# Row-tiled decay spreads, a quarter of two chunks' masked products on GpSimd, and re-placed gate, store and sum steps in a fused SSD and expert-merge kernel

## The chip, the cores and the metric

The kernel runs on one core of a Trainium2 chip. The metric is the device time of one execution in microseconds, as the median of several runs. Everything is in fp32.

## What is computed

The reference has two parts, joined by a reshape. The first is a chunked state-space layer (Mamba-2 SSD) over 4 sequences of 768 tokens with 8 heads of 32 values and a state of 16. Cut to what matters:

```python
L = np.exp(cum[:, :, :, None] - cum[:, :, None, :]) * causal   # decays inside a chunk
M = np.einsum('bhin,bhjn->bhij', Cc, Bc) * L                   # scores times decays
y = M @ xc + (Cc @ state) * exp(cum)
state = decay_full * state + sum_j(Bc[j] x[j] * decay_from_j)
```

The second takes the 3072 tokens of 256 values through four two-layer experts and adds them up with normalized gates:

```python
p = domain_probs / (domain_probs.sum(-1, keepdims=True) + 1e-09)
for e in range(E):
    h = np.maximum(x @ w1[e], 0.0)
    out += p[:, e:e + 1] * (h @ w2[e])
```

## The kernel before

**Tiles.** Tokens come in 24 chunks of 128 (the kernel may choose its own chunk length, since the recurrence is the same). Four chunks, one of each sequence, make a block of 512 tokens; there are six blocks. The experts are worked through in steps: eight steps a block (four experts, two halves of the hidden layer), 48 in all, numbered n. A step forms X and Y banks of the first layer (`fmul`, L480; in steps 0 and 1 `plain_first`, L533), turns them into gated hidden tiles on VectorE (`total`, L503; `gated`, L508; `diff`, L520), and multiplies these with w2 one step later (`smul`, L564; `plain_second`, L552). From step 2 on, a Strassen-like scheme with seven products in place of eight is used. It needs sums of the weight blocks (S1 to S4), which GpSimd makes in the first block (`sum_w1`, L186; `sum_w2`, L194: four operations of 128x256 at L180 to L184 and a store to DRAM for the later blocks, L192 and L198).

**One chunk of the first part.** `masks` (L375, ScalarE) cuts C into two masked copies, ctm. `scores` (L382, TensorE) multiplies them with B, in four row tiles of 32x128 (quarter q of the heads in rows 32q to 32q+31), into four banks g. `spread` (L315, TensorE, chunks 0 to 2 only) spreads the chunk's decay factors `a_q` over all 128 partitions into PSUM; later chunks load the spread factors from DRAM (`load_decays`, L123, from `acut_d`, which `store_decays` writes, L277). `decay_part` (L342) scans them on VectorE into the decay matrix LT (L366), and GpSimd makes the B columns of MT from it (L371). `masked` (L401, VectorE) multiplies g with LT into MT, one quarter of the heads at a time (L407). `outputs` (L411, TensorE) multiplies x with MT into y (L433), and ScalarE copies y into yT (L442) and, for the state, into A (L446 to L449).

For chunk 0, `spread` uses four row tiles (K = 32 rows each) in four banks. For chunks 1 and 2 it uses full 128-row matmuls with the stationary operand `qmask` (L332), two of 128x256 to a bank, two banks.

**The gates.** `turn_gates` (L285) transposes the normalized probabilities (pp, L289), ScalarE copies them to p_sb (L292), and SyncE stores them as p_d. `spread_gate` (L295) spreads the rows of one expert over all partitions (gp, L301), and ScalarE copies the result (L305). Without that tile the first `gated` can't run.

**What sets the order.** Nothing is scheduled by a planner: each engine takes its instructions in the order in which the program calls the functions, and waits on semaphores for its data and its buffers. The calls ahead of the loop over steps are L697 to L770. DMAs take turns on eight semaphores of the hardware queues, whichever engine issues them: an issue waits until the transfer eight turns earlier has landed. PSUM tiles are named by bank (X, Y, acc0 to acc3, and two rotating "att" banks); whoever takes a bank waits for the last reader of what was in it. `turn` (L690) multiplies ones into a bank that nobody reads.

Within a step of the loop (L775 to L869) the weight sums have two places: at mid-step, behind the second parts of the decays (L829 to L834), and at the end of the step (L858 to L863).

Of the kernel before, what the change touches and what calls it, by code (L numbers as in the profile page):

```python
# [8 lines left out]
FP32 = mybir.dt.float32  # L9
# [3 lines left out]
P = 128  # L13
NQ, NT = 4, 2
# [3 lines left out]
def kernel(  # L18
# [38 lines left out]
    nc = tc.nc  # L57
# [15 lines left out]
    SPB = E * JJ  # L73
# [7 lines left out]
    PLAIN = 2  # L81
# [192 lines left out]
    nc.gpsimd.tensor_copy(a_cut, a_sb)  # L274
    nc.gpsimd.memset(a_cut[:, :, 0:1], 0.0)

    def store_decays():  # L277
        nc.scalar.dma_start(
            out=acut_d.rearrange("c h s -> (c h) s").rearrange("(p r) s -> p r s", r=2), in_=a_cut)
        nc.scalar.dma_start(  # L280
            out=ac_d.rearrange("c h s -> (c h) s").rearrange("(p r) s -> p r s", r=2), in_=a_sb)

    gate = {}

# [27 lines left out]

    yT, yS = {}, {}

    def spread(c, halves=(0, 1)):  # L315


        s = st[c]
        if c == 0:
            s["a"] = []  # L320
            for q, (pool, tag) in enumerate(((ps_f, "X"), (ps_f, "Y"), (ps_s, "acc2"), (ps_s, "acc3"))):
                k = slice(32 * q, 32 * q + 32)
                b = pool.tile([P, NT * P], FP32, tag=tag, name="a")
                nc.tensor.matmul(
                    out=b, lhsT=ones[k], rhs=a_q[k, c].rearrange("p t s -> p (t s)"),
                    start=True, stop=True, tile_position=(32 * q, 0))
                s["a"].append(b)
            return
        for i in halves:
            b = ps_f.tile([P, 2, NT * P], FP32, tag="XY"[i], name="a")  # L330
            for q in range(2):
                nc.tensor.matmul(  # L332
                    out=b[:, q], lhsT=qmask[:, 2 * i + q, 0:1].to_broadcast([P, P]),
                    rhs=a_q[:, c].rearrange("p t s -> p (t s)"), start=(q == 0), stop=True,
                    skip_group_check=True)
            s.setdefault("a", []).append(b.rearrange("p q s -> p (q s)"))

    def decays(c):
        for part in range(3):
            decay_part(c, part)  # L340
# [60 lines left out]
    def masked(cs, rs):  # L401
        for r in rs:
            for c in cs:
                q = r ^ 2 * turned_round(c)
                h = slice(NT * q, NT * q + NT)
                s = st[c]
                nc.vector.tensor_mul(s["MT"][:, h, 0:P], s["g"][q], s["LT"][:, h])  # L407

    state = {}

    def outputs(cs):  # L411

        ys = {}
        for c in cs:
            k, i = divmod(c, CPB)
            ys[c] = y = ps_att.tile([P, NT, P + N], FP32, tag="att", name="y")
            if k > 0:
                for a_ in range(2):
                    rows = slice(HALF * a_, HALF * a_ + HALF)
                    to = HALF * (1 - a_ if turned_round(c) else a_)  # L420
                    nc.tensor.matmul(  # L421
                        out=y[to:to + HALF, :, 0:P],
                        lhsT=state[i][1].rearrange("p q d -> p (q d)")[rows, rows],
                        rhs=st[c]["cts"][rows], start=True, stop=False,
                        tile_position=(HALF * a_, to), skip_group_check=True)
        for c in cs:
            s, y = st[c], ys[c]
            k, i = divmod(c, CPB)
            w = P + N if k < NBLK - 1 else P
            for t in range(NT):  # L430
                for q in range(NQ):
                    h = NQ * t + q
                    nc.tensor.matmul(  # L433
                        out=y[32 * q:32 * q + 32, t, 0:w], lhsT=s["xb"][:, h * D:h * D + D],
                        rhs=s["MT"][:, NT * q + t, 0:w], start=(k == 0 and t == 0), stop=True,
                        tile_position=(0, 32 * q), skip_group_check=True)
        for c in cs:
            s, y = st[c], ys[c]
            k, i = divmod(c, CPB)
            if i == 0:  # L440
                yT[k] = ffn.tile([P, NT, BLK], FP32, tag="yT", name="yT")
            nc.scalar.copy(out=yT[k][:, :, i * P:i * P + P], in_=y[:, :, 0:P])  # L442
            if k < NBLK - 1:
                s["A"] = att.tile([P, NT, N], FP32, tag="A", name="A", bufs=4)
                if i % 2:
                    nc.scalar.copy(out=s["A"][:HALF], in_=y[HALF:, :, P:])  # L446
                    nc.scalar.copy(out=s["A"][HALF:], in_=y[:HALF, :, P:])
                else:
                    nc.scalar.copy(out=s["A"], in_=y[:, :, P:])  # L449
# [235 lines left out]


    homes = ((ps_s, "acc0"), (ps_s, "acc1"), (ps_att, "att"), (ps_att, "att"))
    banks = ((ps_s, "acc2"), (ps_s, "acc3"), (ps_s, "acc0"), (ps_s, "acc1"))

    def turn(n, w=4):  # L690

# [4 lines left out]

    turn(1)  # L697
    turn(1, 2)
    spread(0)
    turn(1, 3)  # L700
    masks(0)
    scores([0], homes)
    decays(0)
    masks(1)
    spread(1)
    store_decays()
    masks(2)
    masked([0], range(NQ))
    outputs([0])
    scores([1], banks)  # L710
    decays(1)
    turn_gates(ps_att, "att")
    spread(2, (0,))
    spread_gate(ps_att, "att")
    masked([1], range(NQ))
    outputs([1])
    spread(2, (1,))
    sum_w1(0, 0)
    load_decays(3)
    load_w2(1)  # L720
# [54 lines left out]
    for n in range(PLAIN, NS):  # L775
        k, r = divmod(n, SPB)

        ahead = CPB * (k + 1)
        scanned = [ahead + d for d in {0: [0], 2: [1], 4: [2], 5: [3]}.get(r, [])]
        scored = [ahead + d for d in {3: [0, 1], 6: [2, 3]}.get(r, [])]  # L780
        done = [ahead + d for d in {4: [0, 1], 7: [2, 3]}.get(r, [])]
        if k == NBLK - 1:
            scanned, scored, done = [], [], []
        ending = r == 0 and k > 0
        e = r // JJ
        if r % JJ == 0 and n + JJ < NS:
            load_gate(*divmod(n // JJ + 1, E))
        if PLAIN + 2 < n + 2 < NS:
            load_w1(n + 2)
            load_w2(n + 2)  # L790
        opened(n)
        total(n, 1, "11")
        gated(n, "11", "z11")
        for work in late:
            work()
        if r == 1 and k > 0:
            combine(k - 1, 0)
            combine(k - 1, 1)
        for c in scanned:
            decay_part(c, 0)  # L800
        for c in scored:
            masks(c)
        if k > 0 and 2 <= r < CPB + 2:
            leave(k - 1, r - 2)
        smul(n - 1, 1)
        fmul(n, 6)
        snap(n, 6)
        smul(n - 1, 3)
        if ending:
            keep(k - 1, 0)  # L810
        if done:
            outputs(done)
            states.extend(done)
        fmul(n, 5)
        fmul(n, 7)
        snap(n, 7)
        total(n, 7, "22")
        smul(n - 1, 7)
        smul(n - 1, 5)
        if ending:  # L820
            keep(k - 1, 1)
        gated(n, "22", "z22")
        if r == 1 and k > 0:
            combine(k - 1, 2)
        for c in scanned:
            decay_part(c, 1)
        for c in scored:
            decay_part(c, 2)
        if n == PLAIN:  # L829
            sum_w2(0, 1)  # L830
        elif n == SPB - 4:
            sum_w1(n + 2)
        elif n == SPB - 2:
            sum_w2(n)  # L834
        if n < CPB:
            load_chunk(n + CPB)
        for c in scanned if n >= CPB else []:
            if c + 2 < NCH:
                load_decays(c + 2)
        for c in done:  # L840
            if c + CPB < NCH:
                load_tokens(c + CPB)
                load_heads(c + CPB)
        fmul(n, 3)
        total(n, 6, "12")
        fmul(n, 4)
        gated(n, "21", "X")
        gated(n, "12", "z12")
        if r == SPB - 1 and k < NBLK - 1:
            sums(k + 1)  # L850
        smul(n - 1, 6)
        if scored:
            scores(scored, ((ps_att, "att"), (ps_att, "att"), (ps_f, "Y"), (ps_f, "X")))
            masked(scored, (3, 2, 0, 1))
        smul(n - 1, 2)
        diff(n, "T3", "22", "12")
        smul(n - 1, 4)
        if n == PLAIN:  # L858
            sum_w2(1, 1)
        if n != SPB - 4:  # L860
            sum_w1(n + 2)
        if PLAIN < n != SPB - 3:
            sum_w2(n + 1)  # L863
        diff(n, "T1", "12", "11")
        if r == 1 and k > 0:
            turned_out(k - 1)
        late = [lambda n=n: diff(n, "T2", "22", "T1"), lambda n=n: diff(n, "T4", "21", "T2")]
        if states:
            late.append(lambda c=states.pop(0): carry(c))  # L869
# [48 lines left out]
```

## Time and profile before

| what | value |
|---|---|
| median of 7 runs | 641.62 us (641.24 to 643.39) |
| profiled execution | 642.08 us, span 640.3 us |
| granted TensorE clock | 1.000 |
| TensorE, VectorE busy | 633.4 and 484.0 us |
| ScalarE, GpSimd busy | 118.4 and 108.5 us |
| first X matmul of step 0 | 14.69 us |
| waits of TensorE in the page's sense | 1.2, 1.1 and 0.6 us |

A row of a timeline gives the start in us, the length of the merged piece in us, the engine, the line, the operation, what is written and read, and how many instructions are merged; in square brackets stands the idle time before it and what ended it. One 128x256 fp32 matmul leaves two records. PE is TensorE's matmul, DVE VectorE, ACT ScalarE, POOL GpSimd, SP SyncE; a q behind the name means the engine's instruction queue. A piece's length includes the tail of its last instruction, so pieces overlap a little. In the list of waits a row tells who waited for whom, the total, how often, and the longest.

### The profile page before, as it was taken

Reading aid. Unit: us, or ns where it says so; the run is one execution under the profiler, and the core shown is the slowest. Engines: PE = TensorE matmul, PEld = TensorE weight load, DVE = VectorE, ACT = ScalarE, POOL = GpSimd, SP = SyncE. Lnnn points to the kernel's source line nnn. Section 1 sums busy time; section 2 is a strip of 40 time slices with the busy share of each in tenths; the row PEclk is TensorE's granted clock in tenths of the full one; section 3 lists DMA queues with packets and bytes.
Section 4 is the critical chain, followed back from the end, with each engine's and each line's share of the span. In section 5 each row is a group of like instructions: output and inputs, shape, how many; then the busy total and the mean of one; then the engine's idle time right before and its main releaser. Section 6 shows DMA issues by size and latency. Waiting matters only on the chain.

```text
span 640.3 us, 9224 instructions
## 1 busy us (share of the span) xinstructions
PE 633.4 (99%) x3407; PEld 538.4 (84%) x3407; DVE 484.0 (76%) x809; ACT 118.4 (18%) x257; POOL 108.5 (17%) x157
## 2 busy tenths in 40 slices
PE   8999999999999999999999999999999999999997
PEld 5788878888888888888888888888888888888886
DVE  7869998788777788778688778768877677756555
ACT  3011121212111121122121211122111211111110
POOL 4788575020001002100002000000100000100000
PEclk9999999999999999999999999999999999999999
DMA  6988793865666292656375567639365743147000
GB/s 223 304 323 270 264 339 136 276 224 164 174 210 243 68 373 67 235 169 240 116 275 167 167 192 197 235 119 341 78 226 165 248 148 132 62 148 243 1 1 33
DMA packets 97248, 121.61 MB, mean 190 GB/s; under 512 B 28840, under 2 KB 80436, under 8 KB 97204
## 3 DMA queue, kind: packets, MB, share of 16 engines
q1 hardware_dynamic: 94376, 111.20, 52.8%
q0 software_dynamic: 2304, 9.44, 3.8%
q8 instruction: 27, 0.44, 0.3%
q10 hardware_dynamic: 524, 0.39, 0.2%
q14 instruction: 17, 0.14, 0.1%
HBM read 108.16 MB, written 12.83 MB: 189 GB/s over the span
## 4 chain that ended last, share of the span: by engine, by line
PE 96%; DVE 1%; DMA 1%; SPq 0%; ACT 0%; issue 0%; POOL 0%; ACTq 0%; DVEq 0%; POOLq 0%
PE acc L579 43%; PE X L494 25%; PE Y L494 19%; PE acc L560 2%; PE y L433 2%; PE g L395 2%; PE Y L543 1%; PE X L543 1%; PE y L421 1%; DMA xb<-in_xbc_dram 1%; DVE hT L523 0%; DVE h L516 0%; DVE z L506 0%; DVE LT L366 0%; SPq L152 0%
## 5 line engine op out<-in xcount | busy, mean ns | idle before, releaser
L506 DVE TENSOR_TENSOR z<-Y,snap 128x512 f32<-128x512 f32 x138 | 94.6, 685 | 124.7 <-ACT snap L501 73.7
L579 PE MATMUL acc<-hT,wt 128*128 128x256 f32 x736 | 181.2, 379 | 0.0
L501 ACT COPY snap<-X 128x512 f32<-128x512 f32 x138 | 80.8, 586 | 465.8 <-PE X L494 389.6
L579 PEld LDWEIGHTS acc<-hT,wt 128*128 128x128 f32 x736 | 139.8, 190 | 19.0
L579 PE MATMUL acc<-h,wt 128*128 128x256 f32 x552 | 142.5, 381 | 0.0
L494 PE MATMUL X<-yS,wt 128*128 128x256 f32 x552 | 141.7, 379 | 0.0
L579 PEld LDWEIGHTS acc<-h,wt 128*128 128x128 f32 x552 | 104.1, 190 | 17.1 <-issue 2.3
L494 PEld LDWEIGHTS X<-yS,wt 128*128 128x128 f32 x552 | 104.8, 190 | 14.5 <-issue 0.3
L516 DVE SCALAR_TENSOR_TENSOR h<-z,gate 128x512 f32<-128x512 f32 x138 | 100.2, 726 | 3.5 <-PE acc L560 0.4
L494 PE MATMUL Y<-yT,wt 128*128 128x256 f32 x368 | 94.6, 380 | 1.2 <-DVE z L506 1.2
L494 PEld LDWEIGHTS Y<-yT,wt 128*128 128x128 f32 x368 | 68.7, 190 | 12.4 <-DVE z L506 2.0
L523 DVE TENSOR_TENSOR hT<-h,hT 128x512 f32<-128x512 f32 x92 | 65.2, 708 | 1.8
L523 DVE TENSOR_TENSOR hT<-h,h 128x512 f32<-128x512 f32 x92 | 65.6, 754 | 1.1
L366 DVE TENSOR_TENSOR_SCAN LT<-ab,ident 128x512 f32<-128x512 f32 x42 | 52.1, 1242 | 0.0
L494 PE MATMUL Y<-yS,wt 128*128 128x256 f32 x184 | 48.3, 385 | 0.0
L494 PE MATMUL X<-yT,wt 128*128 128x256 f32 x184 | 47.2, 379 | 0.0
L371 POOL TENSOR_TENSOR MT<-xb,LT 128x128 f32<-128x128 f32 x20 | 8.6, 428 | 206.4 <-DVE LT L366 89.8
L494 PEld LDWEIGHTS Y<-yS,wt 128*128 128x128 f32 x184 | 34.1, 190 | 6.4 <-issue 1.1
L494 PEld LDWEIGHTS X<-yT,wt 128*128 128x128 f32 x184 | 35.0, 190 | 4.8
L516 DVE SCALAR_TENSOR_TENSOR h<-X,gate 128x512 f32<-128x512 f32 x50 | 34.3, 685 | 5.9 <-PE X L494 3.6
L407 DVE TENSOR_TENSOR MT<-g,LT 128x256 f32<-128x256 f32 x96 | 33.0, 416 | 5.9 <-PE g L395 5.9
L352 POOL TENSOR_TENSOR cts<-ctm,dec 128x256 f32<-128x256 f32 x20 | 14.2, 728 | 133.6 <-DVE dec L349 133.6
(96 smaller groups left out, 321.3 us busy)
## 6 DMA issues: line engine op xcount, KB each, us to landing
wt<-in_w_dram SPq DMA_DIRECT2D x112, 256.0 KB
wt<-w_d SPq DMA_DIRECT2D x40, 640.0 KB
wt<-w_d SPq DMA_DIRECT2D x40, 512.0 KB
ab<-acut_d SPq DMA_DIRECT2D x21, 512.0 KB
gate<-p_d SPq DMA_DIRECT2D x23, 256.0 KB
w_d<-wt POOLq DMA_DIRECT2D x8, 640.0 KB, 3.7
wt<-in_w_dram SPq DMA_DIRECT2D x40, 128.0 KB
xb<-in_xbc_dram SPq DMA_DIRECT2D x14, 320.0 KB
```

Source lines behind the costliest of these rows:

```text
L352: nc.gpsimd.tensor_mul(cts, s["ctm"], dec.unsqueeze(1).to_broadcast([HN, NT, P]))
L366: nc.vector.tensor_tensor_scan(out=LT[:, i * w:i * w + w], data0=s["a"][i], data1=ident.rearrange("p h s -> p (h s)")[:, :w], initial=0.0, ...
L395: nc.tensor.matmul(out=g.rearrange("p t s -> p (t s)"), lhsT=s["xb"][k, OBT:OBT + P], rhs=s["ctm"][k].rearrange("p t s -> p (t s)"), start ...
L407: nc.vector.tensor_mul(s["MT"][:, h, 0:P], s["g"][q], s["LT"][:, h])
L433: nc.tensor.matmul(out=y[32 * q:32 * q + 32, t, 0:w], lhsT=s["xb"][:, h * D:h * D + D], rhs=s["MT"][:, NT * q + t, 0:w], start=(k == 0 and ...
L494: nc.tensor.matmul(out=f[bank][:, j], lhsT=wt1[n][:, w, j * P:j * P + P], rhs=rhs, start=(i in (1, 2, 5) and j == 0), stop=(j == JJ - 1), ...
L501: nc.scalar.copy(out=s, in_=first[n]["X"])
L506: nc.vector.tensor_add(z, first[n]["Y"], first[n][i])
L516: nc.vector.scalar_tensor_tensor(out=h, in0=first[n][src], scalar=0.0, in1=g.unsqueeze(1).to_broadcast([P, JJ, HB]), op0=ALU.max, op1=ALU. ...
L523: nc.vector.tensor_sub(h[o], h[x], h[y])
L543: nc.tensor.matmul(out=f[bank][:, j], lhsT=wt1[n][:, w, j * P:j * P + P], rhs=yT[k][:, i, cols], start=(i == 0 and j == 0), stop=(i == 1), ...
L579: nc.tensor.matmul(out=acc[k, u][:, half], lhsT=w2_op(n, w)[:, j], rhs=rhs[:, j], start=(begins and j == 0), stop=(n % SPB == SPB - 1 and ...
```

## The change

Chunks 1 and 2 (the second and third) are spread by four row tiles, as chunk 0 was. A new function `aside` takes one quarter of the masked products of chunks 0 and 1: ScalarE copies the scores g from PSUM to SBUF, and GpSimd multiplies. `store_decays` is split into its two stores, which stand at different places. `turn_gates` moves ahead of the outputs of chunk 0, `spread_gate` behind the scores of chunk 1, ahead of chunk 2's spread. Banks are handed out anew. In the loop, the sums of w2 of steps 5 and 7 move from the end of the step before to the middle of their own step.

```diff
-    def store_decays():
-        nc.scalar.dma_start(
-            out=acut_d.rearrange("c h s -> (c h) s").rearrange("(p r) s -> p r s", r=2), in_=a_cut)
+    def store_decays(kind):
+        d, sb = ((acut_d, a_cut), (ac_d, a_sb))[kind]
         nc.scalar.dma_start(
-            out=ac_d.rearrange("c h s -> (c h) s").rearrange("(p r) s -> p r s", r=2), in_=a_sb)
+            out=d.rearrange("c h s -> (c h) s").rearrange("(p r) s -> p r s", r=2), in_=sb)
...
-    def spread(c, halves=(0, 1)):
+    def spread(c, homes):
...
-        for i in halves:
-            b = ps_f.tile([P, 2, NT * P], FP32, tag="XY"[i], name="a")
-            for q in range(2):
-                nc.tensor.matmul(
-                    out=b[:, q], lhsT=qmask[:, 2 * i + q, 0:1].to_broadcast([P, P]),
-                    rhs=a_q[:, c].rearrange("p t s -> p (t s)"), start=(q == 0), stop=True,
-                    skip_group_check=True)
-            s.setdefault("a", []).append(b.rearrange("p q s -> p (q s)"))
+        s["a"] = []
+        for q, (pool, tag) in enumerate(homes):
+            k = slice(32 * q, 32 * q + 32)
+            b = pool.tile([P, NT * P], FP32, tag=tag, name="a")
+            nc.tensor.matmul(
+                out=b, lhsT=ones[k], rhs=a_q[k, c].rearrange("p t s -> p (t s)"),
+                start=True, stop=True, tile_position=(32 * q, 0))
+            s["a"].append(b)
...
+    def aside(c, q):
+
+        s = st[c]
+        h = slice(NT * q, NT * q + NT)
+        g = att.tile([P, NT, P], FP32, tag="gs", name="gs")
+        nc.scalar.copy(out=g, in_=s["g"][q])
+        nc.gpsimd.tensor_mul(s["MT"][:, h, 0:P], g, s["LT"][:, h])
...
-    banks = ((ps_s, "acc2"), (ps_s, "acc3"), (ps_s, "acc0"), (ps_s, "acc1"))
+    banks = ((ps_f, "X"), (ps_f, "Y"), (ps_s, "acc2"), (ps_s, "acc3"))
...
-    spread(0)
+    spread(0, banks)
     turn(1, 3)
     masks(0)
     scores([0], homes)
     decays(0)
     masks(1)
-    spread(1)
-    store_decays()
+    spread(1, banks)
+    aside(0, 3)
+    masked([0], (2, 0, 1))
+    store_decays(0)
+    turn_gates(ps_att, "att")
+    store_decays(1)
+    outputs([0])
+    scores([1], ((ps_s, "acc0"), (ps_s, "acc1"), (ps_att, "att"), (ps_f, "X")))
+    decays(1)
+    aside(1, 3)
+    spread_gate(ps_att, "att")
+    masked([1], (0, 1, 2))
+    spread(2, ((ps_s, "acc2"), (ps_s, "acc3"), (ps_f, "Y"), (ps_s, "acc0")))
     masks(2)
-    masked([0], range(NQ))
-    outputs([0])
-    scores([1], banks)
-    decays(1)
-    turn_gates(ps_att, "att")
-    spread(2, (0,))
-    spread_gate(ps_att, "att")
-    masked([1], range(NQ))
     outputs([1])
-    spread(2, (1,))
...
-        elif n == SPB - 2:
+        elif n >= SPB - 3:
             sum_w2(n)
...
-        if PLAIN < n != SPB - 3:
+        if PLAIN < n < SPB - 4:
             sum_w2(n + 1)
```

More of the change, by code (lines that the diff above doesn't have):

```diff
@@ L313 @@
     yT, yS = {}, {}
-    def spread(c, halves=(0, 1)):
+    def spread(c, homes):
         s = st[c]
[L319 to L323, printed above, removed]
-                nc.tensor.matmul(
[L325 to L328, printed above, removed]
-        for i in halves:
-            b = ps_f.tile([P, 2, NT * P], FP32, tag="XY"[i], name="a")
-            for q in range(2):
-                nc.tensor.matmul(
-                    out=b[:, q], lhsT=qmask[:, 2 * i + q, 0:1].to_broadcast([P, P]),
-                    rhs=a_q[:, c].rearrange("p t s -> p (t s)"), start=(q == 0), stop=True,
-                    skip_group_check=True)
-            s.setdefault("a", []).append(b.rearrange("p q s -> p (q s)"))
+        s["a"] = []
[6 more added lines that the diff above has]
+            s["a"].append(b)
     def decays(c):
```

## The prediction

> **What bounds the kernel now.** I read the page's first and fourth parts, then TensorE's waits, then the timelines of the first 25 us, then the chain of waits around the one stall outside them.
>
> ```profile
> PE 633.4 (99%) x3407; PEld 538.4 (84%) x3407; DVE 484.0 (76%) x809; ACT 118.4 (18%) x257; POOL 108.5 (17%) x157
> PE 96%; DVE 1%; DMA 1%; SPq 0%; ACT 0%; issue 0%; POOL 0%; ACTq 0%; DVEq 0%; POOLq 0%
> ```
>
> TensorE is busy 99% of the span and carries 96% of the chain that ended last. So the body of the kernel can't get shorter through other engines; only stretches in which TensorE does avoidable work or waits are open. TensorE's waits show how few there are:
>
> ```profile
> PE Y L494 <- DVE z L506: 1.2, 1, 1.2
> PE t L694 <- DVE ones L206: 1.1, 1, 1.1
> PE gp L301 <- ACT p_sb L292: 0.6, 1, 0.6
> ```
>
> The second is the start. The third is in the lead-in, the stretch before the first expert matmul (X, L543), from where TensorE runs without a gap until 87 us. TensorE and ScalarE in it (start, length, what):
>
> ```profile
> 10.22 0.31 PE L289 MATMUL pp<-ident,pr 128*96 128x128 f32 x1
> 10.37 1.03 PE L332 MATMUL a<-a_q,qmask 128*128 128x256 f32 x4
> 12.01 1.16 PE L301 MATMUL gp<-p_sb,ident 96*128 96x128 f32 x8 [0.61 <-ACT p_sb L292]
> 13.09 0.70 PE L433 MATMUL y<-MT,xb 128*32 128x144 f32 x16
> 13.72 1.13 PE L332 MATMUL a<-a_q,qmask 128*128 128x256 f32 x4
> 14.69 1.89 PE L543 MATMUL X<-yT,wt 128*128 128x256 f32 x8
> ```
>
> ```profile
> 9.82 0.32 ACTq L280 DMA_DIRECT2D ac_d<-a_sb  x1
> 10.76 0.69 ACT L380 ACTIVATE ctm<-xb,tmask 128x128 f32<-128x128 f32 x2 [3.15 <-DMA xb<-in_xbc_dram]
> 11.69 0.26 ACT L292 COPY p_sb<-pp 96x128 f32<-96x128 f32 x1
> 13.86 0.37 ACT L442 COPY yT<-y 128x256 f32<-128x256 f32 x1
> ```
>
> p_sb stands on ScalarE behind chunk 2's ctm, which waits for that chunk's tokens to land at 10.7; gp, and behind it chunk 1's y, wait for p_sb. And 0.97 us of L332 lies between y and X.
>
> The first wait is the stall at 88 us (VectorE, GpSimd, TensorE; two VectorE rows of the next step for comparison):
>
> ```profile
> 81.90 1.46 DVE L516 SCALAR_TENSOR_TENSOR h<-z,gate 128x512 f32<-128x512 f32 x1
> 83.28 2.35 DVE L523 TENSOR_TENSOR hT<-h,hT 128x512 f32<-128x512 f32 x2
> 87.64 0.67 DVE L506 TENSOR_TENSOR z<-Y,snap 128x512 f32<-128x512 f32 x1
> 95.50 0.69 DVE L516 SCALAR_TENSOR_TENSOR h<-z,gate 128x512 f32<-128x512 f32 x1
> 96.11 1.41 DVE L523 TENSOR_TENSOR hT<-h,hT 128x512 f32<-128x512 f32 x2
> ```
>
> ```profile
> 82.06 0.74 POOL L180 TENSOR_TENSOR wt<-wt 128x256 f32<-128x256 f32 x1
> ```
>
> ```profile
> 88.36 1.13 PE L494 MATMUL Y<-yT,wt 128*128 128x256 f32 x4 [1.25 <-DVE z L506]
> ```
>
> While GpSimd makes the sums of w2 of step 5 (82.06 to 86.2), the same VectorE operations take 1.46 instead of 0.69 and 2.35 instead of 1.41. The z that must empty bank Y is late, and TensorE stands 1.25 us.
>
> **Row tiles (lead-in).** Removed: eight full matmuls of 128x256 (chunk 1: 6.85 to 8.77, 1.92 us; chunk 2: 1.03 + 0.97 after its pp), added: two sets of four row tiles. Four such tiles took 1.16 us at 3.92 (L324) and 0.65 at 9.57 (L395, same shape); the new sets run after the second, so I take 0.65 and keep 1.16 as the upper end. TensorE work falls by 3.92 - 1.3 = 2.6 us. The Trainium skill (TensorEngine Tiling, "Gotcha 1: PSUM Pressure") speaks against it: row tiles need a bank each, so software has to wait for banks. The row says what that is here: the tiles of chunk 1 reuse the four banks of chunk 0, whose scans end at 5.8, 6.4, 7.0 and 7.6, so the set ends at 7.9, not 7.5; pp and chunk 0's y stand behind it. By row alone y could start at 7.6; with the banks nothing is lost, because y needs masked products that end later.
>
> VectorE: chunk 1's scans become four of 0.59 (2.35 for 2.43, by pitch) instead of 2.24 together: +0.11. Chunk 2's: 2.35 in one piece.
>
> **A quarter of the products on GpSimd.** VectorE loses 0.35 us per chunk. Added: a ScalarE copy 128x256 from PSUM (0.35, L442) and a GpSimd product. The skill (GPSIMD Engine Reference, "Performance versus the Vector engine") calls GpSimd about 2x slower for elementwise work; the rows say 0.72 (L180) against 0.416 (L407), 1.73x. By rule 0.83, by row 0.72; I use 0.72, upper end 1.64 (the longest L184, beside a slowed VectorE). Chunk 0: copy 7.61 to 7.95, L371 7.6 to 8.0, product to 8.7; VectorE's three end at 8.56. y of chunk 0 starts at 8.6 instead of 8.77. Chunk 1: scans 8.56 to 10.91, products to 11.95; GpSimd L371 to 11.35, product to 12.06. The two engines end together, so the added wait costs 0.1 (0.9 at the upper end). Queued behind it on GpSimd are sums of w1 (11.61 before, 12.1 now), for which nobody waits: GpSimd then idles 2.2 us anyway for chunk 2's scan.
>
> **Gates and stores.** The pp transpose moves ahead of y, p_sb ahead of the second store and of chunk 2's ctm. New on ScalarE: yT of chunk 0 is behind the issue of ac_d, which was held until 9.82 (it takes the turn of a weight load that landed then). So: ac_d to 10.14, yT 10.16 to 10.5, A to 10.6, copy for chunk 1 to 10.87. gp takes A's bank: 10.66 to 11.74 (1.08 by pitch). Then chunk 2's spread to 12.39 (its fourth bank is free once chunk 1's first product is read, 11.3), y of chunk 1 to 13.02, yT 13.07 to 13.42, X at **13.45 instead of 14.69: 1.24 us**. Gate copy (to 12.33) and chunk 2's ctm (tokens landed at 10.7, to 12.97) fit ahead of yT. SyncE: p_d's store goes at 10.7 rather than 11.98; the load behind it, chunk 3's decays, waited until 14.08 for acut_d, and still does. It must be there at 18.55 instead of 19.79. In the one-microsecond windows from 14 to 17 us the queues moved 43 + 283 + 194 = 520 KB, and this load has 512, so about 17 us: cover of 1.5 us; without it y of chunk 3 would slip by the rest beyond 0.1 to 0.4 us.
>
> If ac_d's issue were not held, X would start at 13.15 (gain 1.5); if GpSimd's product takes 1.64, at 14.2 (gain 0.5). After X, chunk 2's scans (12.0 to 14.35) end well before the third scores need their bank (15.3). Everything then is the old order 1.24 us earlier, GpSimd too, because it waits for chunk 2's and chunk 3's scans.
>
> **Sums at mid-step.** The built order of GpSimd changes in one place only: w2 of step 5 goes behind L371 of chunk 7, ahead of w1 of step 7. (w2 of step 7 is named later too, but nothing lies between; it runs when it did.) In old times: VectorE after 81.17 loses the excess 0.77 + 0.94 + about 0.2 = 1.9, more than the 1.25 of the stall; z is then ready at 86.7, TensorE free for Y at 87.1: **1.25 us gained**. Its price: L371 and w2 run at 89 to 94, where w1 ran; w1 runs at 94 to 98.2, over h, hT and the carry of step 6. These stretch by up to 1.9 us; VectorE idled 1.39 there (before z at 99.64) and z ended 0.2 before its matmul. So 0 to 0.3 us of new stall; I take 0.15. Moving these sums past nothing on SyncE, and their stores to no load sooner than step 13, costs nothing. Needed by: S4 of w2 at 95.0 against 92.4 made. Net **1.1 us**.
>
> **Sum.** 1.24 + 1.1 = 2.3 us of the profiled execution: 642.08 (span 640.3 plus 1.78 around it) becomes 639.8. It lay 0.46 above the median of the runs, so the forecast is 641.62 - 2.3 = 639.3. A measurement of this kernel tells about 0.2% (1.28 us) from no change.
>
> **Rivals.**
> Only the lead-in pays (0.12). The stall moves with w1 to step 6 instead of vanishing. For: the two sum blocks are back to back there. Against: 1.39 us of VectorE idle, and no scan in that step, where step 5 had one of 1.22. Gives 641.62 - 1.24 = 640.4.
> Only the sums pay (0.14). ScalarE now strings store issue, yT, A, copy, gate, ctm and yT in front of X; each 0.1 us of delay counts. If these or GpSimd's product slip by 1.24, the wait for p_sb is replaced by one for yT or MT: 640.5. Against: my chain has 9.82 from the trace as its start.
> Slower (0.10). TensorE's clock. The skill (TensorE: Matmul & The Clock Gate, "The HAM clock gate") says that an idle window of about 3.4 us halves it until one busy window has passed; less dense work in the lead-in invites that. For: four row tiles at 3.9 us took 1.16, nearly twice 0.65, so a slow start exists though the granted clock reads 1.00 in every row. Against: my gaps are 0.6 (before y), 0.5 (gp) and 0.4 (X). By row nothing is lost; by rule, three windows at half rate lose 5.1 us: 641.62 - 2.3 + 5.1 = 644.4. It decides from 7.2 us at half rate.
>
> The main case has 0.62. **Range** 638.5 (lead-in 1.5, sums 1.25, 0.4 of spread in the runs) to 641.3 (one part pays, with a stall of 0.9). Chances: faster 0.67 (main case, some of the two half cases), same 0.22, slower 0.11.
>
> **What would show it.** L324-like tiles of chunk 1 end at 7.9, of chunk 2 at about 12.4; X's first matmul at 13.45; no TensorE wait at 87, h and hT there 0.69 and 1.4; slowed h and hT in step 6 with at most 0.3 us of wait. Wrong if X starts after 14, if L371 of chunk 7 doesn't hold w2's sums back to 89, or if matmuls of 9 to 16 us are stretched.

## The result and the profile after

The changed kernel takes 640.05 us in the median of 14 runs (639.48 to 640.85); the kernel before took 641.80 in 34 (641.24 to 643.42). The ratio is 0.9971, with a 95% interval of 0.9964 to 0.9978: 1.9 us faster, between 1.4 and 2.3. The profiled execution took 639.86 us at a span of 638.1, 2.2 us under that of before. Four of the 34 executions of the kernel before took 643.2 to 643.4 and none of the changed one more than 640.9; none of these four was profiled, and what slowed them stays open.

The page, first part:

```profile
PE 632.0 (99%) x3407; PEld 536.8 (84%) x3407; DVE 484.0 (76%) x811; ACT 119.0 (19%) x259; POOL 109.7 (17%) x159
```

TensorE's busy time fell by 1.4 us only, although 2.6 us of matmul work were taken out: a row counts as busy while its tiles wait for banks (below, chunk 1's tiles at 6.63 stand at 1.71 us, chunk 2's at 11.62 at 0.71). TensorE's waits:

```profile
PE t L691 <- DVE ones L206: 1.1, 1, 1.1
PE X L540 <- ACT yT L439: 0.5, 1, 0.5
PE gp L300 <- ACT A L446: 0.3, 1, 0.3
```

The wait of 1.2 us on z is gone. In place of the wait of 0.6 us for p_sb there are two, on yT and on A, which together are longer; so what is gained in the lead-in is not the waiting time itself. TensorE and ScalarE there:

```profile
6.63 1.71 PE L322 MATMUL a<-a_q,ones 32*128 32x256 f32 x8
10.53 1.16 PE L300 MATMUL gp<-p_sb,ident 96*128 96x128 f32 x8 [0.33 <-ACT A L446]
11.62 0.71 PE L322 MATMUL a<-a_q,ones 32*128 32x256 f32 x8
12.26 0.70 PE L430 MATMUL y<-MT,xb 128*32 128x144 f32 x16
13.45 1.99 PE L540 MATMUL X<-yT,wt 128*128 128x256 f32 x8 [0.49 <-ACT yT L439]
```

```profile
9.66 0.31 ACTq L279 DMA_DIRECT2D ac_d<-a_sb  x1
10.02 0.37 ACT L439 COPY yT<-y 128x256 f32<-128x256 f32 x1 [1.12 <-DMA wt<-in_w_dram]
13.02 0.37 ACT L439 COPY yT<-y 128x256 f32<-128x256 f32 x1
```

X starts at 13.45 as forecast, by the forecast chain: ac_d's issue, yT, A, gp, chunk 2's row tiles, y, yT. That it agrees to the hundredth is luck: gp and y came 0.13 us earlier than forecast, and the way from y to X took 0.13 longer. VectorE, GpSimd and TensorE in steps 5 and 6:

```profile
80.78 0.69 DVE L513 SCALAR_TENSOR_TENSOR h<-z,gate 128x512 f32<-128x512 f32 x1
81.39 1.41 DVE L520 TENSOR_TENSOR hT<-h,hT 128x512 f32<-128x512 f32 x2
92.86 1.47 DVE L513 SCALAR_TENSOR_TENSOR h<-z,gate 128x512 f32<-128x512 f32 x1
94.25 2.34 DVE L520 TENSOR_TENSOR hT<-h,hT 128x512 f32<-128x512 f32 x2
```

```profile
88.00 0.72 POOL L180 TENSOR_TENSOR wt<-wt 128x256 f32<-128x256 f32 x1
...
93.03 0.74 POOL L180 TENSOR_TENSOR wt<-wt 128x256 f32<-128x256 f32 x1
```

```profile
85.82 1.03 PE L491 MATMUL Y<-yT,wt 128*128 128x256 f32 x4
96.18 1.89 PE L576 MATMUL acc<-hT,wt 128*128 128x256 f32 x8
98.21 1.13 PE L491 MATMUL Y<-yT,wt 128*128 128x256 f32 x4
```

The slow h and hT have moved from step 5 to step 6, with w1 (93.03). By pitch, that is from one start to the next, a record takes 0.216 us; eight of them from 96.18 end at 97.91. Y starts at 98.21, so the new stall is 0.3 us where the old one was 1.4.

### The profile page after: what moved, and what is told of

Same layout as the page of the kernel before. It is cut to its first block, busy times and chain, and to the rows that moved or that the text cites. A ratio compares the mean times of both kernels' runs of the same rounds, so it can differ in the third digit from the quotient of the medians.

```text
span 638.1 us, 9231 instructions
## 1 busy us (share of the span) xinstructions
PE 632.0 (99%) x3407; PEld 536.8 (84%) x3407; DVE 484.0 (76%) x811; ACT 119.0 (19%) x259; POOL 109.7 (17%) x159
## 4 chain that ended last, share of the span: by engine, by line
PE 96%; DVE 1%; DMA 1%; SPq 0%; issue 0%; ACT 0%; POOL 0%; ACTq 0%; DVEq 0%; POOLq 0%
PE acc L576 43%; PE X L491 25%; PE Y L491 19%; PE acc L557 2%; PE y L430 2%; PE g L384 2%; PE X L540 1%; PE Y L540 1%; PE y L418 1%; DMA wt<-in_w_dram 1%; DVE hT L520 0%; DVE h L513 0%; SPq L120 0%; DVE z L503 0%; PE gp L300 0%
## 5 line engine op out<-in xcount | busy, mean ns | idle before, releaser
L491 PEld LDWEIGHTS X<-yS,wt 128*128 128x128 f32 x552 | 104.8, 190 | 14.5 <-issue 0.3
```

Of the source, the lines that this page charges most:

```text
L491: nc.tensor.matmul(out=f[bank][:, j], lhsT=wt1[n][:, w, j * P:j * P + P], rhs=rhs, start=(i in (1, 2, 5) and j == 0), stop=(j == JJ - 1), ...
```

## The experiments

Ratios are to the kernel before, timed in the same rounds, and need not equal a quotient of medians. The first four runs, the next four and the last four were each made on a chip of their own, so across these groups the ratios compare better than the medians.

**The lead-in alone.** The conditions of the sums in the loop as before:

```diff
-        elif n >= SPB - 3:
+        elif n == SPB - 2:
             sum_w2(n)
...
-        if PLAIN < n < SPB - 4:
+        if PLAIN < n != SPB - 3:
             sum_w2(n + 1)
```

> All of the change except the moved weight sums. My theory: two gains that add up. The lead-in alone: X of step 0 starts at 13.45 as with the whole change, TensorE is about 1.1 us ahead from the second X on, and the wait of 1.25 us on z in step 5 is still there, only 1.1 us earlier (near 87). Time 1.1 us under before (about 640.7). Rival (the earlier lead-in shifts VectorE against GpSimd and so removes the stall by itself): no wait above 0.3 us in step 5, 2.2 us under before.

Measured: 641.14 us, ratio 0.9983 (0.9972 to 0.9994), 1.1 us under before. TensorE's row of step 5:

```profile
87.24 1.13 PE L491 MATMUL Y<-yT,wt 128*128 128x256 f32 x4 [1.25 <-DVE z L503]
```

The stall is whole. X started at 13.29, earlier than expected: in this execution ac_d's issue found its transfer landed and went at 8.88.

**The sums alone.** The same lines changed the other way round in the kernel before.

> The kernel before with only the sums of w2 of steps 5 and 7 moved to mid-step. My theory: X of step 0 at 14.69, no wait of TensorE on z in step 5, h and hT there at 0.69 and 1.41 instead of 1.46 and 2.35, a wait of 0.1 to 0.3 us in step 6 instead; 1.1 us under before (about 640.7). Rival (the stall comes back in step 6, because w1 of step 7 now runs there): a wait of 1 us or more in step 6, time within 0.3 us of before.

Measured: 641.21 us, ratio 0.9989 (0.9976 to 1.0003): 0.7 us under before, not clear of none. TensorE, ScalarE and VectorE of its profile:

```profile
12.87 1.16 PE L301 MATMUL gp<-p_sb,ident 96*128 96x128 f32 x8 [1.48 <-ACT p_sb L292]
15.55 1.89 PE L543 MATMUL X<-yT,wt 128*128 128x256 f32 x8
```

```profile
11.63 0.69 ACT L380 ACTIVATE ctm<-xb,tmask 128x128 f32<-128x128 f32 x2 [3.59 <-DMA xb<-in_xbc_dram]
```

```profile
82.73 0.69 DVE L516 SCALAR_TENSOR_TENSOR h<-z,gate 128x512 f32<-128x512 f32 x1
```

The stall of step 5 is gone, and step 6 has 0.3 us, as expected. But X is at 15.55, not 14.69, though the lead-in is that of before: chunk 2's tokens landed 0.9 us later in this execution. The span was 640.0, so behind X this kernel ran 1.2 us less than the one before (624.4 against 625.6). The two parts add up: 1.1 and 0.7 by time, 1.9 together.

**No quarter on GpSimd.** All four quarters of chunks 0 and 1 on VectorE:

```diff
-    aside(0, 3)
-    masked([0], (2, 0, 1))
+    masked([0], (2, 3, 0, 1))
...
-    aside(1, 3)
...
-    masked([1], (0, 1, 2))
+    masked([1], range(NQ))
```

> The whole change, but all four quarters of the masked products of chunks 0 and 1 on VectorE. My theory: the quarter on GpSimd is worth only what VectorE is late by, since the gate chain covers part of it: VectorE ends chunk 1's products at 12.6 instead of 11.9, y of chunk 1 starts there instead of 12.26, X at about 13.75 instead of 13.45; 0.3 us slower than the whole change. Rival (VectorE's chain is what bounds the lead-in): the full two quarters come back, X at about 14.15, 0.7 us slower. Second rival (the quarter does nothing): X at 13.45.

Measured: 640.43 us, ratio 0.9967 (0.9954 to 0.9980), no slower than the whole change. Its TensorE:

```profile
11.30 1.16 PE L300 MATMUL gp<-p_sb,ident 96*128 96x128 f32 x8 [1.00 <-ACT A L446]
12.39 0.71 PE L322 MATMUL a<-a_q,ones 32*128 32x256 f32 x8
13.03 0.70 PE L430 MATMUL y<-MT,xb 128*32 128x144 f32 x16
14.22 1.99 PE L540 MATMUL X<-yT,wt 128*128 128x256 f32 x8 [0.49 <-ACT yT L439]
```

Inconclusive: the transfer that ac_d waits for landed at 10.4, gp came 0.8 us late, and y (13.03) waited for the spread, not for VectorE, whose products had ended at 12.6.

**Full spreads.** Chunks 1 and 2 by the old matmuls with `qmask`, in banks X and Y; the fourth score tile of chunk 1 in acc2:

```diff
-    spread(1, banks)
+    spread_full(1)
...
-    spread(2, ((ps_s, "acc2"), (ps_s, "acc3"), (ps_f, "Y"), (ps_s, "acc0")))
+    spread_full(2)
```

> The whole change, but chunks 1 and 2 spread by full matmuls of 128 rows, as before. My theory: chunk 1's is hidden behind the masked products, chunk 2's lies between gp and y on TensorE and takes 1.9 us instead of 0.65: y of chunk 1 at about 13.5, X at 14.6 to 14.7, 1.1 to 1.2 us slower than the whole change; so the lead-in's whole gain hangs on the row tiles of chunk 2. Rival (the moved gates are what gains): X stays within 0.3 us of 13.45.

Measured: 640.93 us, ratio 0.9983 (0.9971 to 0.9994). Its TensorE:

```profile
10.24 1.16 PE L300 MATMUL gp<-p_sb,ident 96*128 96x128 f32 x8
11.24 1.89 PE L331 MATMUL a<-a_q,qmask 128*128 128x256 f32 x8
14.25 1.99 PE L550 MATMUL X<-yT,wt 128*128 128x256 f32 x8 [0.49 <-ACT yT L449]
```

From gp to X it takes 4.01 us, with row tiles 2.92: 1.1 us, by the spread of chunk 2 alone (y of chunk 0 starts at 8.97 here, 8.52 with tiles, and nothing behind follows from that). By time the full spreads give up about 0.8 us of the 1.9, with intervals that just touch (0.9971 to 0.9994 against 0.9964 to 0.9978). The transfer landed early in this execution, so X at 14.25 is 1.0 behind the lead-in run's 13.29 too.

**The store behind chunk 0's copies.** From here the question was the transfers, which the prediction had taken as fixed.

```diff
-    store_decays(1)
     outputs([0])
+    store_decays(1)
```

> The whole change with one pair of lines swapped: the store of ac_d is issued behind chunk 0's copies of yT and A on ScalarE, not ahead of them. Theory formed on the runs so far: that issue waits for a weight transfer to land (8.9 to 10.4 in three profiles), and gp, chunk 2's spread, y and X of step 0 wait behind it, so X moves with a transfer from one execution to the next. Then here gp follows the scores at 10.1 to 10.2 without a wait, X starts at 13.2 to 13.3 in every execution, 0.2 us under the whole change in the median, and the runs lie closer together than 1.4 us. Rival (the landing is covered and the spread comes from outside the lead-in): X and the spread of the runs as with the whole change.

Measured: 640.55 us (640.09 to 641.07), ratio 0.9972 (0.9962 to 0.9982). No gain; X came at 13.96. Its ScalarE and TensorE:

```profile
11.23 0.32 ACTq L279 DMA_DIRECT2D ac_d<-a_sb  x1
11.59 0.37 ACT L403 COPY gs<-g 128x256 f32<-128x256 f32 x1 [1.51 <-PE gp L300]
```

```profile
12.81 0.68 PE L430 MATMUL y<-MT,xb 128*32 128x144 f32 x10 [0.32 <-POOL MT L404]
```

The moved store now follows the store of p_d and the load of chunk 3's decays in the turns of the DMA semaphores, so it waits for a later weight transfer, to 11.2. Behind it now stands the copy gs for GpSimd's quarter, and y waits for that. The wait had changed its victim.

**The same without the quarter on GpSimd.** The edits of "The store behind chunk 0's copies" and of "No quarter on GpSimd" together.

> As the run with the store behind the copies, but with all four quarters of the masked products on VectorE. With no wait for a transfer in front, my theory gives the GpSimd quarter its price: VectorE ends chunk 1's products at 12.5 to 12.6, y of chunk 1 starts there instead of 12.05, X at 13.7 to 13.8 instead of 13.25: 0.5 us slower than with the quarter on GpSimd. Rival (it is worth nothing, as it looked when the transfer was late): X within 0.1 us of the run with it.

Measured: 640.27 us, ratio 0.9967 (0.9954 to 0.9981). Its TensorE:

```profile
12.38 0.92 PE L430 MATMUL y<-MT,xb 128*32 128x144 f32 x16
13.76 1.99 PE L540 MATMUL X<-yT,wt 128*128 128x256 f32 x8 [0.46 <-ACT yT L439]
```

X at 13.76 as expected, against 13.28 and 13.29 in the three profiles where the quarter is on GpSimd and no transfer holds ScalarE up (lead-in alone, and the two kernels below with the store last). So the quarter is worth 0.5 us of X when transfers are early; when one is late it is covered. By time it can't be told from nothing: 640.27 here and 640.55 with the quarter and the store at the same place, where the store held up the quarter's copy; ratios 0.9967 and 0.9972.

**Both repairs, first form.** The last of the four operations of w1 of step 7 and its store move behind cts of step 6, the store of ac_d as in "The store behind chunk 0's copies":

```diff
         elif n >= SPB - 3:
+            if n == SPB - 2:
+                sum_w1(n + 1, 1)
             sum_w2(n)
...
-            sum_w1(n + 2)
+            sum_w1(n + 2, 0 if n == SPB - 3 else None)
```

> The store behind the copies, and the last of the four operations of w1 of step 7 with its store moved behind cts of step 6. My theory of the moved sums: VectorE is slowed only while GpSimd computes, so 1.2 us less of GpSimd in step 6 takes 0.2 us off the carry (S back to 0.25 from 0.48), and the wait of about 0.17 us of TensorE in step 6 goes; the time equals the run with only the store moved, 0.1 to 0.2 us lower at most. Rival: the wait stays, because z waits for the snapshot anyway.

Measured: 640.36 us (639.46 to 642.63), ratio 0.9976 (0.9963 to 0.9989). VectorE and TensorE in step 6:

```profile
97.21 0.25 DVE L456 SCALAR_TENSOR_TENSOR S<-S,dec 128x32 f32<-128x32 f32 x1
97.71 0.68 DVE L503 TENSOR_TENSOR z<-Y,snap 128x512 f32<-128x512 f32 x1
```

```profile
96.63 1.89 PE L576 MATMUL acc<-hT,wt 128*128 128x256 f32 x8
98.44 1.13 PE L491 MATMUL Y<-yT,wt 128*128 128x256 f32 x4
```

S is back at 0.25 (0.48 with the whole change), and Y follows acc 0.08 us behind its pitch: the step-6 stall is gone, as my theory had it. The time shows nothing of it, because X was at 13.94: TensorE was slow until 9.2 in this execution (more below).

**Chunk 2's ctm ahead.**

```diff
+    masks(2)
     turn_gates(ps_att, "att")
...
-    masks(2)
```

> The whole change, but chunk 2's ctm stands on ScalarE ahead of the gate rows' copy and chunk 0's copies, as before the change. My theory: everything behind waits for chunk 2's tokens to land (10.7 to 11.6): p_sb near 11.4, yT and A to 12.7, gp at 12.7 or later, X at 15.6 to 16.5, later than before the change; with the sums' 1.1 us the time is within 1 us of before. Rival (the order on ScalarE is of no account): X within 0.5 us of 13.45.

Measured: 644.73 us (640.41 to 646.90), ratio 1.0029 (1.0006 to 1.0051). Slower than before, and by something that neither theory had. TensorE, and windows of one and two us (the column ahead of the last two is the granted clock):

```profile
10.75 1.17 PE L384 MATMUL g<-ctm,xb 32*128 32x256 f32 x4 [0.69 <-ACT p_sb L291]
11.85 2.08 PE L300 MATMUL gp<-p_sb,ident 96*128 96x128 f32 x8
16.70 3.78 PE L540 MATMUL X<-yT,wt 128*128 128x256 f32 x8 [0.49 <-ACT yT L439]
```

```profile
10.00:11.00 1.00, 0.31 (x4) 0.25 (x4) 1.00 (x3) 1.00 (x5) 0.41 (x1) 0.92 1.08 346
11.00:12.00 1.00, 1.00 (x5) 0.35 (x3) 0.14 (x2) 0.06 (x2) 0.00 (x0) 0.50 1.02 364
...
20.00:22.00 2.00, 2.00 (x13) 1.10 (x12) 1.23 (x3) 0.00 (x0) 0.39 (x1) 0.73 1.05 361
22.00:24.00 2.00, 2.00 (x27) 1.34 (x25) 1.48 (x4) 0.00 (x0) 0.00 (x0) 1.00 1.08 411
```

The granted clock falls to half at 10.84 (0.92 in that microsecond is 0.16 us at half) and comes back at 21.08 (0.73 over two is 1.08 us at half): 10.24 us. X's four matmuls take 3.78 instead of 1.99. Of eight executions, the four at a mean clock of 0.991 to 0.992 took 645.2 to 646.9 us, two at 0.994 and 0.997 took 644.2 and 644.0, and the two at 0.999 took 640.4 and 641.8.

**The same with a matmul of ones in the wait.** One `turn` of 128x512 into bank Y, which is free there, between the second and third score tile of chunk 1:

```diff
+                if c == 1 and r == 1:
+                    turn(1, 4, ps_f, "Y")
```

> The kernel with chunk 2's ctm ahead (644.7 us in the median, granted clock 0.50 from about 10.9 to 21.2 in its profile), with one matmul of ones, 128x512 into a free bank that nobody reads, in the wait between its second and third score tile. Theory (TensorE was too sparse there, and the clock was halved for three windows): the clock stays at 1.00 in most executions, X's four matmuls take 1.9 us instead of 3.8 and start near 14 to 14.5, and the median falls to 640.5 to 641.5, as its two executions at a clock of 0.999. Rival (the lateness is the order on ScalarE, not the clock): the median stays above 643.

Measured: 642.02 us, ratio 1.0002 (0.9985 to 1.0019). Its TensorE:

```profile
11.01 1.13 PE L693 MATMUL t<-ones 128*128 128x512 f32 x2
12.56 0.70 PE L384 MATMUL g<-ctm,xb 32*128 32x256 f32 x4 [0.43 <-ACT p_sb L291]
16.11 1.99 PE L542 MATMUL X<-yT,wt 128*128 128x256 f32 x8 [0.49 <-ACT yT L441]
```

With added work the median is 2.7 us lower. It comes from another chip; by the ratios the gain is 1.7 us, and their intervals overlap. The clock tells more: ten of twelve executions ran at 0.999 or 1.00 and took 640.8 to 642.5, two at 0.994 and took 645.6, where without the added matmul six of eight lay below 0.999. So most of what that kernel lost was the clock. The rest is the order on ScalarE: the tokens landed at 11.7 here, and X came at 16.1, later than the 14 to 14.5 that I expected, which is why the median lies above my range of 640.5 to 641.5.

**No store ahead of X.** The store of ac_d behind chunk 1's copies:

```diff
-    store_decays(1)
     outputs([0])
...
     outputs([1])
+    store_decays(1)
```

> The whole change with the store of ac_d issued behind chunk 1's copies of yT and A, so that no DMA issue stands on ScalarE ahead of the first X matmul. The run with the store one place later did not gain, because the store took another turn of the DMA semaphores and waited until 11.2 for a later weight transfer, and the copy for GpSimd's quarter waited behind it. Theory: here gp follows the scores at 10.1 to 10.2, y of chunk 1 starts at 12.05 to 12.1, X at 13.2 to 13.3; 0.2 to 0.3 us under the whole change. Rival: ac_d's later landing holds SyncE's load of it (19.3) and the weight loads behind it, and the gain is lost or the time is longer.

Measured: 640.22 us (639.73 to 640.40), ratio 0.9968 (0.9956 to 0.9980); the whole change on the same chip 640.24. X at 13.28 as expected, and no gain in the time. VectorE in steps 0 and 2 and TensorE in step 3:

```profile
19.00 2.34 DVE L355 TENSOR_TENSOR_SCAN LT<-ab,ident 128x512 f32<-128x512 f32 x2 [0.43 <-DMA ab<-acut_d]
45.35 1.25 DVE L513 SCALAR_TENSOR_TENSOR h<-z,gate 128x512 f32<-128x512 f32 x1 [0.42 <-PE acc L557]
```

```profile
58.60 1.13 PE L491 MATMUL Y<-yT,wt 128*128 128x256 f32 x4 [0.33 <-DVE z L503]
```

Chunk 3's scan waited 0.43 us for that chunk's decays to land. GpSimd's part of chunk 3 and the sums queued behind it came 0.5 us later than in the next kernel's profile (21.48 against 20.97), whose program is the same up to step 5 and where the scan waited for nothing. So here a sum lay over h of step 2, which took 1.25 (0.84 with the whole change, 0.81 in the next kernel), and VectorE, without slack through step 3, passed it on: a stall of 0.5 us by pitch. The theory had left this load out, and the rival had named another transfer. As the next kernel has the same store, the stall belongs to this execution's landing, not to the order of the store.

**Both repairs, second form.** That store, and the split of w1.

> The store of ac_d behind chunk 1's copies and the last operation of w1 of step 7 behind cts of step 6: both repairs of the whole change. Theory: X at 13.2 to 13.3 and no wait in step 6; 0.3 to 0.5 us under the whole change (about 639.7), the fastest of all. Rival: no different from the whole change, since the landing of the transfers and the start of the clock move X by as much from one execution to the next.

Measured: 639.62 us (639.40 to 640.05), ratio 0.9961 (0.9949 to 0.9973), 2.5 us under before. X at 13.29, h of step 2 at 0.81, no stall in steps 3, 5 and 6, span 637.6. It is the lowest median, as expected, but its interval overlaps that of the whole change on the same chip.

**The whole change again.**

> The whole change once more, beside the repaired kernels on one chip: the theory of two gains gives 640.0 to 640.2 and no execution above 641.5; the theory that the moved stall and transfers decide would give a median nearer to 640.6.

Measured: 640.24 us (639.71 to 640.39), ratio 0.9968 (0.9957 to 0.9980), nearer to the first theory's 640.0 to 640.2 than to 640.6. Its TensorE:

```profile
6.67 1.34 PE L384 MATMUL g<-ctm,xb 32*128 32x256 f32 x8
...
13.95 1.99 PE L540 MATMUL X<-yT,wt 128*128 128x256 f32 x8 [0.49 <-ACT yT L439]
```

The kernel is the one profiled above; X is 0.5 us later, because TensorE's start lasted longer: the first score tiles took 1.34 here and 0.71 there.

## Why the prediction was right, and where it was off

**Lead-in.** Forecast 1.24, found 1.24 at X's start and 1.1 behind it: X now follows a wait, and its four matmuls take 1.92 to the next start instead of 1.82. The reading of the waits was right: p_sb behind chunk 2's tokens, and chunk 2's spread ahead of X. The moved gates gain little without the row tiles. They brought gp from 12.01 to 10.53, 1.48 us earlier, but put the whole of chunk 2's spread and a wait for yT between gp and X: 2.92 us where it was 2.68. With full spreads this way takes 4.01, so the moved gates without row tiles would have left some 0.15 us (an estimate: 14.69 less 10.53 and 4.01).

**Banks and the quarter on GpSimd.** The row tiles' waits for banks cost nothing that shows: chunk 1's set ended at 8.28, later than the 7.9 forecast, but y of chunk 0 started at 8.52, forecast 8.6. GpSimd's product took 0.73 against the 0.72 assumed. What the quarter is worth had no number in the prediction; it is 0.5 us of X or nothing, according to a transfer.

**Chunk 3's decays.** The prediction let this load land at about 17 us, with 1.5 us to spare. With the whole change VectorE didn't wait for it, but in the run with the store last the scan waited until 19.0. So the cover can be nothing.

**Sums.** Forecast 1.25 - 0.15 = 1.1, found 1.1, but as a difference of two mis-sized terms. By pitch the stall cost 1.41 and 0.1 more in the first set of matmuls behind it, so 1.5; the new one costs 0.3 + 0.1 = 0.4. The idle time in brackets leaves out the tail of the last matmul and the refill, some 0.25 us a wait. Both terms lacked the same piece, and so it cancelled.

**The sum.** 2.3 forecast, 2.2 in the pair of profiles, 1.9 (1.4 to 2.3) by the ratio. The term that failed is the step from the profiled execution to the median: I took one execution's landings as the kernel's. The execution profiled before lies 0.3 us above the median of 34 runs, and the one profiled after 0.2 below its own. The profiles with the whole change have X at 13.45 and 13.95, those with the lead-in of before at 14.69 and 15.55; the difference of two single draws is uncertain by half a microsecond or more. (The chances given to the four cases add up to 0.98.)

**The slower rival.** It didn't come true for this change, but I gave it the wrong ground. I argued that waits of 0.4 to 0.6 us can't halve the clock. In the kernel with ctm ahead the longest wait that the profile lists between the start and the fall was 0.69 us (about 1.0 by pitch, an estimate), and it fell. It does so in the kernel before too: five of the 84 executions timed beside the experiments had a mean clock of 0.997, and took 644.5 to 644.8 us. The Trainium skill (TensorE: Matmul & The Clock Gate, "The HAM clock gate") puts the window at 3413 ns; the 10.24 us at half rate are three of these. The rule as the prediction has it needs one busy window for the way back, so its three were an assumption, which this one profile bears out. Its 5.1 us compare with 4.7 between that kernel's four executions at 0.991 to 0.992 (645.8 in the mean) and its two at 0.999 (641.1); what was sized wrong was not the price but what brings it on. But an idle window, as the page words it, wasn't needed: in the 3.4 us before the fall the matmuls there amount to some 1.5 us by pitch (y 0.65, two score tiles 0.35, pp and a part of chunk 1's tiles), an estimate. The whole change has about 2 us in the same time before gp, also an estimate, and its clock stayed. Where between the two the limit lies, and whether the amount of work alone decides, was not measured.

## What to carry over

A lead-in that hangs on DMA landings took a different time in one execution and the next: ask of each issue, on every engine, which earlier transfer it waits for and what stands behind it, and compare several executions before trusting half a microsecond. Thinning out TensorE's work can cost more than it saves: one order of this lead-in brought the mean clock below 0.999 in six of eight executions. A matmul of ones in the wait brought that to two of twelve; it is worth trying, not a guarantee. GpSimd work is best placed by what VectorE does at that time, not by when its result is needed, and any shift of the two against each other reopens the question.

## What was not expected of the hardware

The clock fell to half when TensorE had been at work for nearly half of the last 3.4 us (the estimate above), and stayed there for 10.24 us. Near the start TensorE ran at about half its pace until 5 to 9 us, according to the execution (score tiles at 1.34 against 0.71 at 6.7 us), while the granted clock read 1.00 in every row. VectorE operations with both inputs in SBUF slowed beside GpSimd, h from 0.69 to 1.46, the hT from 0.69 to 1.16 in the mean and S from 0.25 to 0.48; one with an input in PSUM didn't (h from bank X at 87.97 in the changed kernel took 0.68 beside GpSimd's operation at 88.00); nor did every one with two SBUF inputs (h from z at 88.56: 0.71, while GpSimd's own operation from 88.80 took 1.06 instead of 0.72).
